# GpSimd's share of a sparse-attention stage: thresholds to VectorE, splits behind the masks, VectorE's order written out

## The chip, the cores and the metric

One Trainium2 chip, one core of it. The metric is the device time of one execution, in microseconds (us). The engines are TensorE (PE; its weight loads are listed apart as PEld), VectorE (DVE), ScalarE (ACT), GpSimd (POOL) and SyncE (SP), which issues most DMAs.

## The reference

Three stages follow one another. Attention over q, k, v of shape 4 batches x 8 heads x 576 tokens x 64, where each row of scores keeps only what lies within tau = 0.02 of its maximum:

```
scores = q @ k.T / sqrt(64)
thresh = max(scores, -1) - tau
scores = where(scores >= thresh, scores, -1e9)
attn   = exp(scores - max(scores, -1));  attn /= sum(attn) + 1e-9
x      = attn @ v                       # then 2304 tokens x 512
```

Then a gated stage, `(silu(x @ w_gate) * (x @ w_val)) @ w_out` with 1536 hidden columns, and a bilinear one, `((x @ w1) * (x @ w2)) @ w3 @ w_out2` with 1024. The change lies in attention.

## The kernel before, in words

**Precision.** TensorE runs on a rounded 32-bit type, so each operand is split into a high part (the rounded value) and a low part (the rest), and products are summed over two or three of the combinations. Many VectorE, ScalarE and GpSimd operations are such splits.

**Tiles.** Attention works on 16 head pairs (4 batches x 4), and in each on nine tiles of 128 query rows by 576 keys: four per head, and one (i = 4) that takes the last 64 rows of both heads. That makes 144 tiles, numbered n. For each tile:

- `mm_scores` (lines 426 to 444): four matmuls of 288 columns (eight for i = 4) into one of two score banks `s_bank`.
- `el_max` (475): VectorE negates the scores from the bank into the SBUF tile P and leaves their minimum (the negated maximum) in column c of `stat`.
- `el_thr` (466): GpSimd adds tau to that column. It does so for two tiles at a time (one for i = 4), 80 operations.
- `el_exp` (485): ScalarE makes E = exp(maximum - score) in one of three SBUF buffers (`N_E`).
- `el_mask` (494): VectorE compares P with the threshold, multiplies by E, writes P in place and sums it. It reads two SBUF tiles.

**Transposes.** When tile 4 and tile 8 of a pair are masked, items are queued (`a_items` 629, `b_items` 633): ten that transpose four blocks of P each into a PSUM bank (`it_T`, `it_lq`, `it_kl`), one for the corner, and four that multiply by V (`it_pv`). `evac_split` (506) takes a bank out by one of three paths, which `PATHS` (33) deals out in turn: X, high part by ScalarE and low part by VectorE, put off by one item through `deferred`; Z, high part by ScalarE, then TensorE subtracts it in the bank (`less`, 331) and ScalarE copies the low part; Y, ScalarE copies the bank into SBUF and GpSimd makes both parts (`split_pool`, 100: a rounding at line 101, a subtraction at 104).

**For the next pair**, items in the queue `prep` transpose k and q (`it_k`, `it_q`, through `turn`, 337: ScalarE's high part, VectorE's low part at 343, and then `stack`, 348, which issues SP DMAs into the tiles L and R that the scores read), and the last 64 rows (`it_left`, 407). GpSimd splits V (`split_v`, 301) and, once per batch, the last rows (`split_left`, 284).

**Order.** The loop at lines 705 to 741 goes tile by tile: exponential of n, maximum of n + 1, scores of n + 2, threshold of n, mask of n - 2 (`N_THR`), and between these `some` (693) runs items of the two queues, about two of `main` and one of `prep` per tile. This is only the order in which the program is written: a planner then orders each engine's instructions by their estimated costs and due times. In the last pair (`in_tail`) the path row is `LAST`, and the x loads of the gated stage (`x_prep`, 817) begin. In pairs 3, 6 and 9 (`EARLY`) one early weight unit is converted (`conv_bits` 132, `conv_value` 154), which takes ScalarE, GpSimd (line 151) and VectorE (158).

Of the kernel before, what the change touches and what calls it, by code (L numbers as in the profile page):

```python
# [29 lines left out]

PATHS, LAST = "XZYXZZYXZ", "XZ"


@with_exitstack
def kernel(
# [21 lines left out]
    nc = tc.nc  # L59
# [174 lines left out]
    def attention(actx, early, tail):  # L234
# [33 lines left out]
        def load(p, which):  # L268
            b, hp = divmod(p, HP)
            for i in which if p < NP else ():  # L270
# [10 lines left out]
                        nc.sync.dma_start(out=t, in_=src.rearrange("h (p t) d -> p t h d", t=4))  # L281
                raws[p, i] = t

        def split_left(b):
            qk, vl = lraw.pop(b)
            qks = sp.tile([P, H, 3, D], F32R, tag="qkls", name="qkls", bufs=1)
            eng = nc.gpsimd if b else nc.vector
            for e in (0, 2):
                eng.tensor_scalar(
                    out=qks[:, :, e, :], in0=qk, scalar1=1.0, scalar2=1.0,  # L290
                    op0=ALU.mult, op1=ALU.mult,
                )
            eng.tensor_tensor(
                out=qks[:, :, 1, :], in0=qk, in1=f32(qks[:, :, 0, :]), op=ALU.subtract
            )
            for h in range(2):
                r = slice(64 * h, 64 * h + 64)
                split_pool(VLZ[b % 2][r, :, h, 0, :], VLZ[b % 2][r, :, h, 1, :], vl[r])
# [38 lines left out]
        def turn(raw, hi, lo, scale, then):  # L337

            bank = t_bank()
            turn_p(bank, [raw[:, t, :, :].rearrange("p h d -> p (h d)") for t in range(4)])  # L340
            nc.scalar.activation(out=hi, in_=bank, func=ACTF.Copy, scale=scale)

            nc.vector.scalar_tensor_tensor(  # L343
                out=lo, in0=bank, scalar=scale, in1=f32(hi), op0=ALU.mult, op1=ALU.subtract
            )
# [60 lines left out]

        def it_left(p):
            b, hp = divmod(p, HP)
            L, R = qk_tiles(p)
# [12 lines left out]
            scaled(R[:, 512:640].rearrange("p (h c) -> p h c", h=2), bv[:, 1, :, 64:P])  # L422
            scaled(R[:, 2 * S:2 * S + 64], bv[:, 1, 1, 64:P])
# [70 lines left out]
        def el_mask(p, i, e):  # L494
            b = p // HP
            c = col_of(p, i)
            t = p_tile(p, i)
            nc.vector.scalar_tensor_tensor(  # L498
                out=t, in0=t, scalar=stats[b][:, 1, c:c + 1], in1=e, op0=ALU.is_le, op1=ALU.mult,
                accum_out=sums[b][:, c:c + 1],  # L500
            )
# [1 line left out]

        path_i = [0]

        def evac_split(hi, lo, bank):
            path = LAST[path_i[0] % len(LAST)] if in_tail else PATHS[path_i[0] % len(PATHS)]
            path_i[0] += 1
            if path == "Z":
                nc.scalar.copy(out=hi, in_=bank)  # L510

                def rest():
                    less(bank, hi)
                    nc.scalar.copy(out=lo, in_=bank)

                deferred.append(rest)
            elif path == "X":
                nc.scalar.copy(out=hi, in_=bank)
                deferred.append(
                    lambda: nc.vector.tensor_tensor(  # L520
                        out=lo, in0=bank, in1=f32(hi), op=ALU.subtract
                    )
                )
            else:
                raw = tmp()
                rv = raw
                if len(bank.shape) == 3:
                    rv = raw.rearrange("p (a c) -> p a c", a=bank.shape[1])
                if len(bank.shape) == 4:
                    rv = raw.rearrange("p (c h q) -> p c h q", c=4, h=2)  # L530
                nc.scalar.copy(out=rv, in_=bank)
                if path == "Y":
                    split_pool(hi, lo, rv)
                else:
                    nc.scalar.copy(out=hi, in_=bank)
                    nc.gpsimd.tensor_tensor(out=lo, in0=rv, in1=f32(hi), op=ALU.subtract)

        def it_T(p, h, c):
            bank = t_bank()
            o = 640 * h + c * P  # L540
            turn_p(bank, [pbuf[p, t][:, o:o + P] for t in range(4)])
            evac_split(AT[h][:, 0, c, 0:512], AT[h][:, 1, c, 0:512], bank)

        def it_lq(p):
            bank = t_bank()
            turn_p(bank, [pbuf[p, 4][:, c * P:(c + 1) * P] for c in range(4)])
            evac_split(
                *(ATT[:, :, e, :, 512:S].rearrange("p h c q -> p c h q") for e in range(2)),
                bank.rearrange("p (c h q) -> p c h q", c=4, h=2),
            )  # L550

        def it_kl(p):
            bank = t_bank()
            turn_p(bank, [pbuf[p, t][:, 512:640] for t in range(4)])
            evac_split(ATL[:, 0, 0:512], ATL[:, 1, 0:512], bank)

        def it_corner(p):
            bank = t_bank()
            nc.tensor.transpose(bank[:, 0:P], pbuf[p, 4][:, 448:S], ident)
            nc.tensor.transpose(bank[0:64, 64:64 + P], pbuf[p, 4][:, 512:S], ident)  # L560
            src, hi = bank[:, 64:P], ATL[:, 0, 512:S]
            nc.scalar.copy(out=hi, in_=src)
            nc.vector.tensor_tensor(
                out=ATL[:, 1, 512:S], in0=src, in1=f32(hi), op=ALU.subtract
            )

        xs_t = {}

        def it_pv(p, h, n):
            flush()  # L570
            b, hp = divmod(p, HP)
            vs = splits[p, 2]
            bank = t_bank()
            w = HALF
# [52 lines left out]
            return [lambda: split_left(p // HP)] if p % HP == 0 else []  # L627

        def a_items(p):
            r = [lambda: split_v(p)] + [lambda c=c: it_T(p, 0, c) for c in range(4)]  # L630
            return r

        def b_items(p):
            r = [lambda: it_kl(p), lambda: it_corner(p)]
# [45 lines left out]
                el_max(*tiles[n], banks.pop(n))  # L680

        def stage_mask(n):
            if n >= 0:
                p, i = tiles[n]
                el_mask(p, i, es.pop(n))
                if i == 4:
                    main.extend(a_items(p))
                if i == 8:
                    main.extend(b_items(p))

        credit = [0.0, 0.0]

# [6 lines left out]
                    run_item(qu.popleft())  # L699
                credit[c] = min(credit[c], 1.0)  # L700

        stage_s(0)
        stage_s(1)
        stage_max(0)
        for n, (p, i) in enumerate(tiles):
            b, hp = divmod(p, HP)
            if i == 0:
                if p + 2 < NP:
                    if (p + 2) % HP == 0:
# [4 lines left out]
                if p + 1 < NP:  # L714
                    prep.extend(prep_items(p + 1))
                    credit[1] = 0.0 if p else -1.5
            if i == NTILE - 2:
# [4 lines left out]
            some(0.4)  # L722
            es[n] = el_exp(p, i)
            stage_max(n + 1)
            stage_s(n + 2)
            el_thr(p, i)
            some(0.3)
            if n >= N_THR:
                stage_mask(n - N_THR)
            some(0.3)  # L730
# [6 lines left out]
            if n + 2 == NS:  # L737
# [4 lines left out]
        for n in range(NS - N_THR, NS):  # L742
# [6 lines left out]
        flush()  # L749

    make_identity(nc, ident)
    nc.vector.tensor_copy(out=ident_r, in_=ident)
# [373 lines left out]
```

## Time and profile before

| | us |
|---|---|
| median of 3 runs | 1181.99 |
| lowest and highest | 1175.48 to 1184.32 |
| the profiled execution: its span, the only time given of it | 1178.8 |
| VectorE busy in the span | 750.1 (64%) |
| TensorE busy in the span | 1113.3 (94%) |
| ScalarE, GpSimd busy in the span | 578.1 (49%), 439.7 (37%) |

The shares of the whole span mix attention (to some 365 us) with two stages of dense matrix work. How long an operation holds its engine is read from the distance between two starts: a VectorE operation and its follower overlap in the records, so durations add up to more than the time that passes.

### The profile page before, as it was taken

How to read it: one execution, taken by the hardware profiler on the slowest of the kernel's cores; microseconds unless marked ns; L12 is line 12 of the kernel's file. 1: busy time of each engine (PE TensorE's matmuls, PEld its weight loads, DVE VectorE, ACT ScalarE, POOL GpSimd, SP SyncE). 2: the span in 40 equal slices, each digit the busy share in tenths (PEclk: the TensorE clock that was granted, in tenths of full speed). 3: DMA queues.
4: the chain of work that ended last, by engine and by line, in shares of the span. 5: the costliest groups of instructions: out<-in, count | busy, mean ns of one | idle time of the engine just before them, and what ended most of it. 6: DMA issues, size and time to landing. Idle time of an engine off the chain costs nothing.

```text
span 1178.8 us, 16730 instructions
## 1 busy us (share of the span) xinstructions
PE 1113.3 (94%) x6044; PEld 952.0 (81%) x6044; DVE 750.1 (64%) x1320; ACT 578.1 (49%) x1041; POOL 439.7 (37%) x431
## 2 busy tenths in 40 slices
PE   6898879899988899999999999999899999999998
PEld 5787769788876778888888888888787888888886
DVE  7999898999886786665472655477891122522222
ACT  5787876888876455443232433344662231321111
POOL 4365454555444555443241432333242221321110
PEclk9999999999999999999999999999999999999999
DMA  8865674766555832221120120123330010100023
GB/s 189 194 146 131 145 177 112 167 147 137 121 175 141 257 99 87 89 72 55 35 71 19 54 72 19 52 92 102 113 108 18 1 36 1 36 1 1 1 60 101
DMA packets 105330, 107.07 MB, mean 91 GB/s; under 512 B 48288, under 2 KB 79648, under 8 KB 105248
## 3 DMA queue, kind: packets, MB, share of 16 engines
q1 hardware_dynamic: 105104, 106.01, 34.2%
q8 instruction: 47, 0.77, 0.3%
q14 instruction: 35, 0.29, 0.1%
q10 hardware_dynamic: 144, 0.00, 0.0%
HBM read 68.16 MB, written 14.23 MB: 70 GB/s over the span
## 4 chain that ended last, share of the span: by engine, by line
PE 64%; DVE 19%; DMA 8%; issue 3%; POOL 2%; SPq 2%; ACT 2%; DVEq 0%; ACTq 0%; POOLq 0%
PE t_bank L830 36%; PE s_bank L830 19%; DVE P L498 5%; DVE P L479 4%; PE t_bank L579 4%; PE s_bank L440 2%; DMA raw<-in_moe_w_dram 2%; DMA slot<-x_dram 1%; PE t_bank L326 1%; DVE slot L813 1%; DMA slot<-r_dram 1%; DVE tmp L158 1%; DVE tmp L146 1%; DVE AT L520 1%; DMA L<-qlo 1%
## 5 line engine op out<-in xcount | busy, mean ns | idle before, releaser
L830 PE MATMUL t_bank<-slot,slot 128*128 128x512 f32 (+1 forms) x2592 | 559.9, 371 | 5.6 <-DVE slot L813 1.8
L830 PEld LDWEIGHTS t_bank<-slot,slot 128*128 128x128 f32 x2592 | 457.5, 189 | 91.7 <-DVE slot L813 2.7
L830 PE MATMUL s_bank<-h,slot 128*128 128x512 f32 (+1 forms) x720 | 161.0, 371 | 7.4 <-DVE slot L877 4.2
L151 POOL TENSOR_TENSOR raw<-raw 128x512 int32<-128x512 int32 x76 | 83.9, 1104 | 189.0 <-ACT raw L150 165.3
L830 PEld LDWEIGHTS s_bank<-h,slot 128*128 128x128 f32 x720 | 126.4, 190 | 31.9 <-ACT tmp L914 3.2
L498 DVE SCALAR_TENSOR_TENSOR P<-P,stat,E 128x576 f32<-128x576 f32 x144 | 142.0, 999 | 11.8 <-POOL stat L471 10.6
L1062 DVE TENSOR_TENSOR tmp<-tmp,t_bank 128x512 f32<-128x512 f32 (+1 forms) x40 | 25.4, 634 | 178.3 <-PE t_bank L830 178.3
L488 ACT ACTIVATE E<-P,stat 128x576 f32<-128x576 f32 x144 | 113.6, 791 | 27.9 <-DVE P L479 25.2
L108 POOL TENSOR_TENSOR h<-tmp,h 128x512 fp32r<-128x512 f32 (+1 forms) x60 | 74.5, 1242 | 128.8 <-ACT h L107 128.6
L479 DVE TENSOR_SCALAR_CACHE_REDUCE P<-s_bank,neg 128x576 f32<-128x576 f32 x144 | 115.0, 808 | 10.3 <-PE s_bank L440 9.8
L1066 POOL TENSOR_TENSOR h<-tmp,h 128x512 fp32r<-128x512 f32 (+1 forms) x38 | 45.8, 1206 | 200.8 <-ACT h L1064 200.8
L440 PE MATMUL s_bank<-R,L 128*128 128x288 f32 x512 | 100.0, 317 | 19.3 <-DVE P L479 12.6
L830 PE MATMUL s_bank<-slot,h 128*128 128x512 f32 x432 | 106.6, 391 | 0.9 <-DVE slot L1052 0.8
L915 DVE TENSOR_TENSOR tmp<-tmp,t_bank 128x512 f32<-128x512 f32 (+1 forms) x60 | 37.9, 631 | 107.2 <-PE t_bank L830 100.5
L440 PEld LDWEIGHTS s_bank<-R,L 128*128 128x128 f32 x512 | 74.6, 191 | 33.8 <-DVE P L479 24.2
L326 PE MATMUL t_bank<-ident,P 128*128 128x128 f32 x640 | 91.4, 279 | 6.3 <-DVE klo L343 1.3
L830 PEld LDWEIGHTS s_bank<-slot,h 128*128 128x128 f32 x432 | 79.9, 188 | 18.3 <-DVE slot L1052 2.1
L158 DVE SCALAR_TENSOR_TENSOR tmp<-tmp,raw 128x512 f32<-128x512 f32 x76 | 69.5, 915 | 39.3 <-POOL raw L151 39.3
L877 DVE TENSOR_TENSOR slot<-s_bank,slot 128x1024 f32<-128x1024 f32 (+1 forms) x72 | 82.5, 1147 | 18.5 <-PE s_bank L830 16.5
L149 ACT ACTIVATE raw<-raw,ebias 128x512 int32<-128x512 int32 x76 | 58.0, 764 | 61.9 <-DVE tmp L146 48.2
L914 ACT ACTIVATE tmp<-t_bank 128x512 f32<-128x512 f32 (+1 forms) x60 | 33.3, 555 | 110.0 <-PE t_bank L830 104.3
L326 PEld LDWEIGHTS t_bank<-ident,P 128*128 128x128 f32 x640 | 74.3, 142 | 13.6 <-DVE klo L343 2.0
(103 smaller groups left out, 1397.8 us busy)
## 6 DMA issues: line engine op xcount, KB each, us to landing
raw<-in_moe_w_dram SPq DMA_DIRECT2D x32, 512.0 KB, 3.6
raw<-in_moe_w_out_dram SPq DMA_DIRECT2D x20, 512.0 KB, 3.6
x_dram<-xs SPq DMA_DIRECT2D x64, 144.0 KB, 2.4
L<-qlo SPq DMA_DIRECT2D x60, 128.0 KB, 2.4
L<-qhi SPq DMA_DIRECT2D x60, 128.0 KB, 4.0
raw<-in_moe_w_gate_dram SPq DMA_DIRECT2D x12, 512.0 KB, 4.3
raw<-in_moe_w_val_dram SPq DMA_DIRECT2D x12, 512.0 KB, 4.5
ld<-in_k_dram SPq DMA_DIRECT2D x16, 256.0 KB, 3.4
```

The lines of the kernel that those rows point to most:

```text
L108: nc.gpsimd.tensor_tensor(out=lo, in0=src, in1=f32(hi), op=ALU.subtract)
L149: nc.scalar.activation(out=a, in_=x, func=ACTF.Relu, scale=8.0, bias=ebias[:, 0:1])
L151: nc.gpsimd.tensor_tensor(out=a, in0=a, in1=x, op=ALU.subtract)
L158: nc.vector.scalar_tensor_tensor(out=f32(m), in0=f32(m), scalar=2.0 ** 20, in1=f32(a), op0=ALU.add, op1=ALU.mult)
L326: nc.tensor.matmul(bank[:, t * P:(t + 1) * P], lhsT=part, rhs=ident, is_transpose=True, start=(t == 0), stop=(t == len(parts) - 1),)
L440: nc.tensor.matmul(o, lhsT=lhs, rhs=R[:, c:c + HALF], start=(h == hs2[0] and e == 0), stop=(h == hs2[-1] and e == 1),)
L479: nc.vector.tensor_scalar(out=p_tile(p, i).rearrange("p (a c) -> p a c", a=2), in0=sb[:, :, 0:HALF], scalar1=neg, scalar2=None, op0=ALU.mu ...
L488: nc.scalar.activation(out=e, in_=p_tile(p, i), func=ACTF.Exp, scale=-1.0, bias=stats[p // HP][:, 0, c:c + 1],)
L498: nc.vector.scalar_tensor_tensor(out=t, in0=t, scalar=stats[b][:, 1, c:c + 1], in1=e, op0=ALU.is_le, op1=ALU.mult, accum_out=sums[b][:, c: ...
L579: nc.tensor.matmul(o, lhsT=vs[:, 4 * h + c, :, :].rearrange("p a d -> p (a d)"), rhs=AT[h][:, e, c, cs], start=(c == 0 and e == 0), stop=F ...
L830: nc.tensor.matmul(o, lhsT=lhs(a), rhs=rhs(c), start=(first and i == 0), stop=(last and i == 2))
L877: nc.vector.tensor_tensor(out=a, in0=s, in1=a, op=ALU.add)
```

## The change

- **Thresholds.** `el_thr` becomes one VectorE operation of one column for every tile (144).
- **Rounds of two tiles.** The loop goes in rounds: both maxima, both thresholds, both exponentials, the scores of the next two tiles, then the masks of the two tiles of the round before (`LAG` = 2). Items run before the maxima and on both sides of the masks, as many per tile as before.
- **VectorE's order.** Under `manual_schedule` VectorE runs in the order in which the program is written, from the first round until before the last pair; the planner still orders the other engines.
- **GpSimd's splits** are no longer issued where they arise but queued in `pool_q`, each with a cost. After the masks of a round, `pool_room` issues as many as fit in `ROOM` = 1.95 us, and each of these waits (by a semaphore) for the round's second mask. `pool_need` issues what is left, without that wait, before an item that reads it.
- **Paths.** Even pairs take YYZXZXZXZX, odd pairs YYZXZXZXZZ over their ten banks.
- **Low parts** of k and q (with their DMAs) and of the corner are put off by one item, as path X's already were. `split_v` moves from the first item of `a_items` to the start of its pair.

```diff
-N_THR, N_E = 2, 3
+LAG, N_E = 2, 3
+ROOM = 1.95
-PATHS, LAST = "XZYXZZYXZ", "XZ"
+PATHS, LAST = ("YYZXZXZXZX", "YYZXZXZXZZ"), "XZ"
...
+        def pool_next(gate=None):
+            _, cost, piece = pool_q.popleft()
+            made = piece()
+            if gate is not None and cost:
+                tc.add_manual_dep(
+                    made.ins, gate.ins.name,
+                    mybir.DependencyInfo(mybir.DependencyClass.Sync, mybir.DependencyReason.DATA),
+                    reason="behind the masks",
+                )
+        def pool_room(gate):
+            room = ROOM
+            while pool_q and pool_q[0][1] <= room:
+                room -= pool_q[0][1]
+                pool_next(gate)
+        def pool_need(*tags):
+            while any(t in tags for t, _, _ in pool_q):
+                pool_next()
+        def p_round(tag, hi, src, cost=0.62):
+            pool_q.append((tag, cost, lambda: nc.gpsimd.tensor_scalar(
+                out=hi, in0=src, scalar1=1.0, scalar2=1.0, op0=ALU.mult, op1=ALU.mult
+            )))
+        def p_rest(tag, lo, src, hi, cost=1.29):
+            pool_q.append((tag, cost, lambda: nc.gpsimd.tensor_tensor(
+                out=lo, in0=src, in1=f32(hi), op=ALU.subtract
+            )))
...
         def split_v(p):
-            split_pool(t[:, :, 0, :], t[:, :, 1, :], raw.rearrange("p h t d -> p (h t) d"))
+            p_round(("v", p), t[:, :, 0, :], src)
+            p_rest(("v", p), t[:, :, 1, :], src, t[:, :, 0, :])
             splits[p, 2] = t
-            load(p + 2, (2,))
+            pool_q.append((("v", p), 0.0, lambda: load(p + 2, (2,))))
...
-            nc.vector.scalar_tensor_tensor(
-                out=lo, in0=bank, scalar=scale, in1=f32(hi), op0=ALU.mult, op1=ALU.subtract
-            )
-            then()
+            def rest():
+                nc.vector.scalar_tensor_tensor(
+                    out=lo, in0=bank, scalar=scale, in1=f32(hi), op0=ALU.mult, op1=ALU.subtract
+                )
+                then()
+            deferred.append(rest)
...
-            if i in (0, 2, 5, 7):
-                return
-            c = slice(col_of(p, i) - (i != 4), col_of(p, i) + 1)
-            nc.gpsimd.tensor_scalar(
+            c = slice(col_of(p, i), col_of(p, i) + 1)
+            nc.vector.tensor_scalar(
                 out=st[:, 1, c], in0=st[:, 0, c], scalar1=tau_sb, scalar2=None, op0=ALU.add
             )
...
+        for n in round_of(0):
+            stage_s(n)
+        order = ExitStack()
+        order.enter_context(tc.manual_schedule(engines={mybir.EngineType.DVE}))
+        for n in range(0, NS, 2):
+            if n + NTILE + 1 == NS:
+                order.close()
+            for m in round_of(n):
+                begin_tile(m)
+            some(0.5)
+            for m in round_of(n):
+                stage_max(m)
+            for m in round_of(n):
+                el_thr(*tiles[m])
+            for m in round_of(n):
+                es[m] = el_exp(*tiles[m])
+            for m in round_of(n + 2):
+                stage_s(m)
+            some(0.75)
+            masks = [stage_mask(m) for m in round_of(n - LAG)]
+            if masks:
+                pool_room(masks[-1])
+            some(0.75)
+            for m in round_of(n):
+                end_tile(m)
```

Not shown: path Y and the splits of the last rows through the same two helpers, `pool_need("qk")` at the head of `it_left`, `pool_need(("v", p), ("vl", b), "at")` in `it_pv`, and the old loop's statements moved into `begin_tile` and `end_tile`.

## Rows read from the trace of the kernel before

**Rows 1.** Page, part 2: VectorE's busy tenths in 40 slices

```profile
DVE  7999898999886786665472655477891122522222
```

**Rows 2.** Table by stage: length, busy us of PE, PEld, DVE, ACT, POOL; PEclk, DMA, GB/s

```profile
38.10:348.00 309.90, 278.29 (x2009) 253.31 (x2009) 285.00 (x643) 249.91 (x499) 163.57 (x190) 0.99 0.63 147
...
450.00:1178.80 728.80, 719.17 (x3447) 604.39 (x3445) 357.18 (x499) 251.62 (x410) 210.41 (x176) 1.00 0.16 51
```

**Rows 3.** Line 479, maxima: ns shortest, median, longest; first and last start

```profile
L479 DVE TENSOR_SCALAR_CACHE_REDUCE P<-s_bank,neg x144: 800/807/819, 17.6 to 343.7; 128x576 f32<-128x576 f32 x144
```

**Rows 4.** Costliest groups, 30 to 330 us: busy us, mean ns, idle before and releasers

```profile
L498 DVE SCALAR_TENSOR_TENSOR P<-P,stat,E 128x576 f32<-128x576 f32 x132 | 130.8, 1003 | 10.1 <-POOL stat L471 8.9 <-ACT E L488 0.5 <-ACT xs L591 0.4
```

**Rows 5.** Line 498, masks, whole run, and what VectorE idled for before them

```profile
L498 DVE SCALAR_TENSOR_TENSOR P<-P,stat,E x144: 800/814/1931, 20.4 to 348.8; 128x576 f32<-128x576 f32 x144
...
  POOL stat L471: 10.6, 14
```

**Rows 6.** Timeline near 199 us: start, duration, engine, line, operation

```profile
198.28 0.81 DVE L479 TENSOR_SCALAR_CACHE_REDUCE P<-s_bank,neg 128x576 f32<-128x576 f32 x1
...
198.91 1.29 POOL L104 TENSOR_TENSOR AT<-tmp,AT 128x512 fp32r<-128x512 f32 x1
...
199.02 1.81 DVE L498 SCALAR_TENSOR_TENSOR P<-P,stat,E 128x576 f32<-128x576 f32 x1
```

**Rows 7.** Line 520, low parts of path X, whole run

```profile
L520 DVE TENSOR_TENSOR AT<-t_bank,AT x50: 628/680/692, 27.8 to 364.7; 128x512 fp32r<-128x512 f32 x50
```

**Rows 8.** Lines 101 and 104, GpSimd's splits of path Y, whole run

```profile
L101 POOL TENSOR_SCALAR AT<-tmp x29: 609/622/1192, 27.7 to 331.2; 128x512 fp32r<-128x512 f32 x29
...
L104 POOL TENSOR_TENSOR AT<-tmp,AT x29: 1272/1292/1892, 28.4 to 332.5; 128x512 fp32r<-128x512 f32 x29
```

**Rows 9.** Timeline, VectorE, near 5 us: an operation of one column and its follower

```profile
5.45 0.15 DVE L656 TENSOR_SCALAR neg<-tau_sb 128x1 f32<-128x1 f32 x1
5.51 0.69 DVE L392 TENSOR_SCALAR slot<-ld 128x256 fp32r<-128x256 f32 x3
```

**Rows 10.** Timeline, 211 to 217 us: q's high part, its low part and the follower

```profile
211.65 0.61 ACT L341 ACTIVATE qhi<-t_bank 128x512 fp32r<-128x512 f32 x1
...
216.35 0.68 DVE L343 SCALAR_TENSOR_TENSOR qlo<-t_bank,qhi 128x512 fp32r<-128x512 f32 x1
216.95 0.68 DVE L520 TENSOR_TENSOR ATL<-t_bank,ATL 128x512 fp32r<-128x512 f32 x1
```

**Rows 11.** Line 440, scores: what TensorE and its loads idled for (us, times)

```profile
  DVE P L479: 40.6, 72
  DMA L<-qlo: 5.2, 9
```

**Rows 12.** Timeline, ScalarE, near 301 us

```profile
300.78 0.78 ACT L488 ACTIVATE E<-P,stat 128x576 f32<-128x576 f32 x1
301.46 0.58 ACT L518 CAST AT<-t_bank 128x512 fp32r<-128x512 f32 x1
```

**Rows 13.** Timeline, TensorE, 226 to 229 us

```profile
226.48 1.03 PE L326 MATMUL t_bank<-ident,P 128*128 128x128 f32 x8
227.27 1.30 PE L440 MATMUL s_bank<-R,L 128*128 128x288 f32 x8
228.41 1.03 PE L326 MATMUL t_bank<-ident,P 128*128 128x128 f32 x8
```

**Rows 14.** VectorE's waits, whole run: us in total, times, longest

```profile
DVE P L479 <- PE s_bank L440: 9.8, 10, 1.9
...
DVE klo L343 <- ACT khi L341: 4.2, 1, 4.2
```

**Rows 15.** Timeline, GpSimd and VectorE, 91 to 94 us

```profile
91.59 1.60 POOL L104 TENSOR_TENSOR sp<-ld,sp 128x512 fp32r<-128x512 f32 x1
...
91.97 1.26 DVE L602 TENSOR_SCALAR r<-sums 128x36 f32<-128x36 f32 x1
93.27 0.38 DVE L605 RECIPROCAL r<-r 128x36 f32<-128x36 f32 x1
```

More of the change, by code (lines that the diff above doesn't have):

```diff
@@ L286, in split_left @@
             qks = sp.tile([P, H, 3, D], F32R, tag="qkls", name="qkls", bufs=1)
[L287 to L291, printed above, removed]
-                )
-            eng.tensor_tensor(
-                out=qks[:, :, 1, :], in0=qk, in1=f32(qks[:, :, 0, :]), op=ALU.subtract
-            )
+            if b:
+                for e in (0, 2):
+                    p_round("qk", qks[:, :, e, :], qk)
+                p_rest("qk", qks[:, :, 1, :], qk, qks[:, :, 0, :])
+            else:
+                for e in (0, 2):
+                    nc.vector.tensor_scalar(
+                        out=qks[:, :, e, :], in0=qk, scalar1=1.0, scalar2=None, op0=ALU.mult
+                    )
+                nc.vector.tensor_tensor(
+                    out=qks[:, :, 1, :], in0=qk, in1=f32(qks[:, :, 0, :]), op=ALU.subtract
+                )
             for h in range(2):
                 r = slice(64 * h, 64 * h + 64)
-                split_pool(VLZ[b % 2][r, :, h, 0, :], VLZ[b % 2][r, :, h, 1, :], vl[r])
+                hi, lo = (VLZ[b % 2][r, :, h, e, :] for e in range(2))
+                p_round(("vl", b), hi, vl[r], 0.42)
+                p_rest(("vl", b), lo, vl[r], hi, 0.74)
             lsplit[b] = qks
@@ L408, in it_left @@
             b, hp = divmod(p, HP)
+            pool_need("qk")
             L, R = qk_tiles(p)
@@ L467, in el_thr @@
             st = stats[p // HP]
-            if i in (0, 2, 5, 7):
-                return
-            c = slice(col_of(p, i) - (i != 4), col_of(p, i) + 1)
-            nc.gpsimd.tensor_scalar(
+            c = slice(col_of(p, i), col_of(p, i) + 1)
+            nc.vector.tensor_scalar(
                 out=st[:, 1, c], in0=st[:, 0, c], scalar1=tau_sb, scalar2=None, op0=ALU.add
@@ L504, in attention, with evac_split @@
         path_i = [0]
-        def evac_split(hi, lo, bank):
-            path = LAST[path_i[0] % len(LAST)] if in_tail else PATHS[path_i[0] % len(PATHS)]
+        def evac_split(p, hi, lo, bank):
+            row = LAST if in_tail else PATHS[p % 2]
+            path = row[path_i[0] % len(row)]
             path_i[0] += 1
@@ L531, in evac_split @@
                 nc.scalar.copy(out=rv, in_=bank)
[L532 to L536, printed above, removed]
+                p_round("at", hi, rv)
+                p_rest("at", lo, rv, hi)
         def it_T(p, h, c):
@@ L541, in it_T @@
             turn_p(bank, [pbuf[p, t][:, o:o + P] for t in range(4)])
-            evac_split(AT[h][:, 0, c, 0:512], AT[h][:, 1, c, 0:512], bank)
+            evac_split(p, AT[h][:, 0, c, 0:512], AT[h][:, 1, c, 0:512], bank)
         def it_lq(p):
@@ L547, in it_lq @@
             evac_split(
-                *(ATT[:, :, e, :, 512:S].rearrange("p h c q -> p c h q") for e in range(2)),
+                p, *(ATT[:, :, e, :, 512:S].rearrange("p h c q -> p c h q") for e in range(2)),
                 bank.rearrange("p (c h q) -> p c h q", c=4, h=2),
@@ L554, in it_kl @@
             turn_p(bank, [pbuf[p, t][:, 512:640] for t in range(4)])
-            evac_split(ATL[:, 0, 0:512], ATL[:, 1, 0:512], bank)
+            evac_split(p, ATL[:, 0, 0:512], ATL[:, 1, 0:512], bank)
         def it_corner(p):
@@ L629, in a_items @@
         def a_items(p):
-            r = [lambda: split_v(p)] + [lambda c=c: it_T(p, 0, c) for c in range(4)]
-            return r
+            return [lambda c=c: it_T(p, 0, c) for c in range(4)]
         def b_items(p):
@@ L682, in stage_mask @@
         def stage_mask(n):
[L683 to L689, printed above, removed]
+            p, i = tiles[n]
+            made = el_mask(p, i, es.pop(n))
+            if i == 4:
+                main.extend(a_items(p))
+            if i == 8:
+                main.extend(b_items(p))
+            return made
         credit = [0.0, 0.0]
@@ L700, in some, with begin_tile @@
                 credit[c] = min(credit[c], 1.0)
[L702 to L706, printed above, removed]
+        def begin_tile(n):
+            p, i = tiles[n]
             if i == 0:
@@ L721, in attention, with end_tile @@
                     prep.extend(split_items(p + 2))
[L722 to L730, printed above, removed]
+        def end_tile(n):
+            p, i = tiles[n]
             if i == 4 and p in EARLY:
@@ L741, in attention, with round_of @@
                 prep.extend(tail())
-        for n in range(NS - N_THR, NS):
+        def round_of(n):
+            return [m for m in (n, n + 1) if 0 <= m < NS]
+        for n in round_of(0):
[23 more added lines that the diff above has]
+                end_tile(m)
+        for n in range(NS - LAG, NS):
             stage_mask(n)
@@ L749, in attention @@
         flush()
+        assert not pool_q
     make_identity(nc, ident)
```

12 lines of the change are left out of this document (8 added, 4 removed).

## The prediction

> **What bounds the kernel now.** I read the page's slices first, then a table by stage, the costliest VectorE groups, and single stretches of the timeline. The slices show VectorE at nine tenths or near it through attention, the first twelve slices, and at a half or less behind it [rows 1]. The stage table says the same: from 38.1 to 348.0 us VectorE is busy 285.0 of 309.9 us, TensorE 278.3, ScalarE 249.9, GpSimd 163.6; behind 450 us TensorE is busy 719.2 of 728.8 [rows 2]. So the change, which touches attention alone, is worth what it takes off VectorE's time there, until TensorE takes over. The 144 maxima start from 17.6 to 343.7 us [rows 3]: 326.1/143 = 2.28 us per tile, 20.5 us per head pair of nine tiles.
>
> The second thing to see is that the masks are longer than they need be. 132 of them have a mean of 1003 ns [rows 4], but the median of all is 814 and the shortest 800 [rows 5]; the maxima, of the same 576 columns, lie between 800 and 819 [rows 3]. The long ones lie beside GpSimd: a mask that starts at 199.02, 0.11 us after a GpSimd subtraction of 1.29 us, lasts 1.81 us and ends 0.6 us after that subtraction does [rows 6]. The mask reads two SBUF tiles (P and E); the low-part subtractions read a PSUM bank, as the maxima do, and keep to 628 to 692 ns through all of this [rows 7]. Third, VectorE stood 14 times, 10.6 us in all, for the threshold that GpSimd computes [rows 5].
>
> **The change part by part.** The sum is made against the profiled span of 1178.8 us, beside which no other time of that execution is given; the median of the three runs is 3.2 us above it, and is what I forecast.
>
> *Masks free of GpSimd.* The splits are released by the second mask of a round and take 0.62 + 1.29 us [rows 8]. VectorE then does two maxima at a step of 0.74 us (198.28 to 199.02) [rows 6], the subtractions that are due, and two thresholds: at least 1.5 us of work that the rows show undisturbed. The stretch above the median goes: 144 x (1003 - 814) ns = 27.2 us. Bounds: 0, if the splits slip into the next masks again, and 27. I take 27, since 1.91 us of splits meet at least 1.5 us of cover and in most rounds a subtraction besides.
>
> *The wait for GpSimd's threshold* goes entirely: 10.6 us. Late next is E from ScalarE, for which a mask stood once in attention, 0.5 us [rows 4]; a mask now comes a whole round behind its exponential.
>
> *144 thresholds on VectorE*, one column each. A row of that size on VectorE lasts 0.15 us but takes a step of 0.06 (5.45 to 5.51) [rows 9]. Low end 144 x 0.06 = 8.6 us. The high end is a threshold that waits for its own accumulator and takes its full 0.15 us: 21.6. I take 0.08 us, near the row, since the second maximum lies between the first threshold and its accumulator: 11.5 us added.
>
> *Paths.* Three or four of ten banks take path X where three of nine did: 3.5 against 3.33 per pair, 0.17 x 16 x 0.60 us (a low part's step, 216.35 to 216.95 [rows 10]) = 1.6 us more on VectorE. ScalarE's copies stay the same within 0.1 per pair.
>
> *Low parts of k, q and the corner put off by one item*, and with k and q the 12 DMAs that their stack calls issue on SP. One item is some 0.7 us (2.28 us per tile, some three items). But before, the planner let a low part lie: qhi's copy began at 211.65 and took 0.61 us, and qlo started at 216.35, 4.1 us after its end [rows 10]. The fixed order puts it one item behind. Bounds: 15 x 0.7 = 10 us lost, if the scores wait for L in each pair, and 5 us gained, what TensorE stood for L [rows 11]. I take 0.
>
> *The new waits.* Behind a gated split on GpSimd lie the later splits and the weight conversion's subtractions, and for these a VectorE operation (line 158) whose place is now fixed. There are three such conversions inside attention: bounds 0 and 3 x 4 us (a round each); I take 2, nearer to nothing because a split is over in 1.9 us. The v split's customer, P times V, comes some two rounds later than the split. The v load on SP moves with its split, earlier; nothing waits for it. On ScalarE, three E buffers now hold the two tiles still to be masked and one new one: the second exponential of a round waits for the round's first mask, and what is queued behind it (copies of banks) waits with it. By steps ScalarE needs 9 exponentials at a step of 0.68 us (300.78 to 301.46) and 16.5 copies at 0.48 (the same 0.10 us of overlap off their 0.58) [rows 12], four of about 0.29 and 0.7 us of small ones per pair: 15.9 us, 3.5 per round of two tiles, in a cadence of 4.2. Up to 0.7 us per round is hidden; the wait is 0 where the planner puts copies ahead of the exponential, and some 0.9 us where it doesn't (second maximum's end to the mask's end, 0.15 + 0.74). I take 0 and keep 72 x (0.9 - 0.7) = 14 us as its upper end.
>
> *What TensorE gives back.* Its steps: transposes 0.10 us (eight from 226.48 to 227.27), scores 0.14 (eight from there to 228.41) [rows 13]; by their columns P times V 0.14 as well and the corrections of path Z 0.14 x 512/288 = 0.25 (estimates). Per pair 50 x 0.10 + 80 x 0.14 + 4.5 x 0.25 + 0.4 for the left block = 17.7 us. VectorE by steps, before: 18 x 0.74 + (3.33 + 2) x 0.60 + 0.14 = 16.7, with the masks' 1.7 and the waits' 0.7 19.1 of the 20.5; 1.4 is norms, conversions and other waits. After: 16.8 + 0.7 for thresholds + 1.4 = 18.9. TensorE's share of the cadence rises from 86% to 94%. VectorE stood 9.8 us for score banks at the lower share [rows 14]; I add half again, 5 us.
>
> Sum: 27 + 10.6 - 11.5 - 1.6 - 0 - 2 - 0 - 5 = 17.5 us saved. I take attention's end to be passed on whole: from 450 us on TensorE is full, and the loads between are started by attention's end. 1178.8 - 17.5 = 1161.3, and with 3.2 us **1164.5 us**.
>
> **A rule that speaks against it.** The norm's first operation, a VectorE tensor_scalar from SBUF to SBUF of 36 columns, took 1.26 us at 91.97, until a GpSimd split that began at 91.59 was over, and its follower started at its end [rows 15]. The Trainium skill, page "SBUF — State Buffer", section "Who interferes with whom", says that a tensor_scalar between SBUF tiles can enter a mode that takes the port pair shared with GpSimd for the whole instruction, and that whoever comes second stands still. The row agrees for 36 columns; no row has one column beside a split. By the rule the thresholds would stand, and the time would be the second rival's.
>
> **The rivals.**
> 1. *TensorE takes it back.* For it: scores waited 40.6 us for maxima [rows 11], so the two are closely coupled; against it: a bank is now asked for a round ahead. If VectorE stands 0.25 us more per round, 72 x 0.25 = 18 us; with the 5 already counted 13 more: 1177.
> 2. *Thresholds stand behind splits,* as the norm's operation did. They come 1.5 us behind the release in a round without a subtraction between, and splits last until 2.0 or so: up to 0.5 us in the 56 rounds that carry a split (3.5 per pair), 28 us at most; in half of them a subtraction has used that time up. Of the 14 us left some would have been waiting anyway: 10 us, 1174.
> 3. *Slower: the fixed order.* A subtraction whose copy is late now holds everything behind it on VectorE, where the planner would have moved a maximum forward; and the copy is late where it is queued behind the second exponential. The longest wait for a copy was 4.2 us, though a single one, at the start [rows 14]. One of 0.6 us in each of 72 rounds costs 43 us: 1164.5 + 43 = 1207. It decides from 17.5/72 = 0.24 us per round. Against it: the copy has an item's time, 0.7 us, for its 0.6.
> 4. *More than forecast.* If thresholds cost their step alone, half of the 1.4 us of other waits goes and TensorE keeps up, a pair takes 16.8 + 0.5 + 0.7 = 18.0 instead of 20.5 us: 16 x 2.5 = 40 us, 1142.
>
> **How the numbers follow.** Forecast 0.45 (its own range 1152 to 1172), rival 1 0.17, rival 2 0.13, rival 3 0.15, rival 4 0.10. What a measurement of this kernel can tell from no change is about 1%, so 1170 to 1194 is the same. Faster: nearly all of the forecast, rival 4 and a third of rival 2's spread, 0.59; within 1%: rival 1 and most of rival 2, 0.26; slower: rival 3, 0.15. The range holds rivals 1 and 2 and the ends of the unknown costs, and leaves out most of rival 3 and half of rival 4: 1142 to 1186.
>
> **What would show it.** Right: masks with a mean below 850 ns; no GpSimd thresholds and no wait of a mask for GpSimd; 144 thresholds of 0.15 us or less; the maxima from first to last in some 308 us instead of 326.1; splits at 0.62 and 1.29 us; at most 15 us of waits of maxima for score banks. Wrong: thresholds of 0.5 us beside splits (rival 2), waits for banks above 25 us (rival 1), subtractions that wait for ScalarE in most rounds (rival 3), or masks still near 1.0 us, in which case the gate does not do what it says.

## The result: slower by 0.6%, and the profile after

The changed kernel takes 1189.04 us (1186.75 to 1191.43) against 1181.6 us before: a ratio of 1.0063, with an interval of 1.0052 to 1.0073. That is within the 1% that my prediction counts as no change, but it lies on the side that I had not forecast and above the end of my range, 1186. The profiled span is 1185.6 us.

The three groups of VectorE in the profile after, by line (ns shortest, median, longest; first and last start). Line 521 is the maxima [rows 3], 540 the masks [rows 5], 513 the thresholds:

```profile
L521 DVE TENSOR_SCALAR_CACHE_REDUCE P<-s_bank,neg x144: 797/810/820, 15.4 to 355.2; 128x576 f32<-128x576 f32 x144
...
L540 DVE SCALAR_TENSOR_TENSOR P<-P,stat,E x144: 799/809/1851, 18.9 to 361.3; 128x576 f32<-128x576 f32 x144
...
L513 DVE TENSOR_SCALAR stat<-stat,tau_sb x144: 195/206/212, 16.9 to 359.7; 128x1 f32<-128x1 f32 x144
```

From the first maximum to the last pass 339.8 us, where 326.1 passed before. A table of just these stretches (length, then busy us of PE, PEld, DVE, ACT, POOL) tells where the 13.7 us came from. The kernel before:

```profile
17.60:343.70 326.10, 290.93 (x2076) 261.63 (x2076) 302.88 (x685) 261.58 (x519) 167.84 (x197) 0.99 0.65 150
```

and after:

```profile
15.40:355.20 339.80, 301.64 (x2120) 272.96 (x2118) 301.76 (x833) 267.81 (x526) 117.75 (x126) 0.96 0.64 148
```

VectorE's busy time is the same, 302.9 and 301.8 us. Its idle time rose from 23.2 to 38.0 us, by 14.8. So two things went wrong at once: the work taken off it came back as other work, and it now stands (waits for an input) longer.

The work came back as thresholds. The timeline of one round, GpSimd's row put among VectorE's:

```profile
217.12 1.29 POOL L313 TENSOR_TENSOR AT<-tmp,AT 128x512 fp32r<-128x512 f32 x1
...
217.12 0.81 DVE L521 TENSOR_SCALAR_CACHE_REDUCE P<-s_bank,neg 128x576 f32<-128x576 f32 x1
...
217.85 0.33 DVE L513 TENSOR_SCALAR stat<-stat,tau_sb 128x1 f32<-128x1 f32 x2
218.10 0.68 DVE L563 TENSOR_TENSOR AT<-t_bank,AT 128x512 fp32r<-128x512 f32 x1
```

Two thresholds take 0.25 us from start to the follower's start, 0.125 each, and 144 of them 18 us. The masks gave 144 x (999 - 839) ns = 23.0 us (the pages' means over all 144), so the gate did what it says; a few late masks, which run beside GpSimd's work for the gated stage (line 883, held by no gate), are still up to 1.85 us long. Two more low parts on path X (58 for 56) and conversions that now meet GpSimd take most of the rest.

The idle time shows in the list of waits from 30 to 330 us (who waited for whom: us in total, times, longest):

```profile
DVE P L521 <- PE s_bank L484: 16.8, 24, 3.8
ACT E L530 <- DVE P L540: 15.5, 17, 4.3
...
DVE AT L563 <- ACT AT L561: 9.0, 9, 1.9
...
PEld t_bank L462 <- POOL qkls L313: 8.1, 3, 2.8
...
DVE klo L384 <- ACT khi L381: 4.6, 4, 1.2
DVE tmp L159 <- POOL raw L152: 3.8, 3, 2.7
...
DVE slot L201 <- ACT slot L198: 2.3, 1, 2.3
```

VectorE stood for GpSimd's threshold before [rows 4]; that is gone. In its place it stands for score banks (16.8 us in this stretch), for ScalarE's copies (9.0 + 4.6) and for the early conversions (3.8 + 2.3). The second line is the wait that I had put at nothing: ScalarE holds the second exponential of a round until a mask frees an E buffer. The fourth is TensorE standing for the last rows' splits, which sit in the queue behind the masks.

Why a copy is late shows in path X's longest wait of this stretch: ScalarE works without a break, and an exponential and another copy stand ahead of the copy that is waited for.

```profile
264.13 0.85 ACT L530 ACTIVATE E<-P,stat 128x576 f32<-128x576 f32 x1
264.81 0.65 ACT L553 CAST AT<-t_bank 128x512 fp32r<-128x512 f32 x1
265.27 0.67 ACT L561 CAST AT<-t_bank 128x512 fp32r<-128x512 f32 x1
...
265.98 0.69 DVE L563 TENSOR_TENSOR AT<-t_bank,AT 128x512 fp32r<-128x512 f32 x1 [1.92 <-ACT AT L561]
```

The worst place is in pair 6, where an early conversion runs. Its steps in the timeline, [idle before <- releaser] at the end:

```profile
156.20 1.04 POOL L152 TENSOR_TENSOR raw<-raw 128x512 int32<-128x512 int32 x1 [4.72 <-ACT raw L151]
...
157.27 0.69 DVE L159 SCALAR_TENSOR_TENSOR tmp<-tmp,raw 128x512 f32<-128x512 f32 x1 [2.75 <-POOL raw L152]
...
159.57 0.63 ACT L198 CAST slot<-tmp 128x512 fp32r<-128x512 f32 x1
160.23 1.09 DVE L201 TENSOR_TENSOR slot<-tmp,slot 128x512 fp32r<-128x512 f32 x1 [2.27 <-ACT slot L198]
...
162.12 1.52 PE L484 MATMUL s_bank<-R,L 128*128 128x288 f32 x8 [2.10 <-DVE P L521]
165.31 2.29 PE L484 MATMUL s_bank<-R,L 128*128 128x288 f32 x8 [1.67 <-DVE P L521]
```

VectorE waits 2.75 us for GpSimd and 2.27 for ScalarE with its maxima and masks queued behind; TensorE then stands 2.10 and 1.67 us, and 2.18 more for the last rows at 169.78. Eight matmuls in 2.29 us, where the line above has 1.52, show the second cost, the clock; the table's granted clock is the third number from the end:

```profile
160.00:165.00 5.00, 1.54 (x9) 1.12 (x8) 4.77 (x12) 3.22 (x6) 1.17 (x2) 0.94 0.97 232
165.00:170.00 5.00, 2.51 (x10) 2.17 (x10) 5.00 (x15) 1.81 (x3) 2.35 (x4) 0.50 0.96 207
170.00:175.00 5.00, 5.00 (x26) 4.93 (x26) 4.11 (x13) 2.37 (x6) 1.95 (x4) 0.54 0.64 140
```

At 0.50 TensorE runs at 1.2 of its 2.4 GHz, for almost 10 us, behind 5 us in which it was busy 1.54. In the kernel before, the lowest 5 us of attention are these:

```profile
295.00:300.00 5.00, 3.87 (x21) 3.41 (x21) 5.00 (x14) 3.97 (x9) 1.41 (x2) 0.77 0.94 203
```

Not all of attention's 13.7 us reach the end: the last maximum starts 11.5 us later, the span is 6.8 us longer. By then TensorE had done 2165 matmuls where it had done 2122 before; behind that point it is busy 811.0 us instead of 813.8 and idle 19.4 instead of 21.3. Over the whole span TensorE's idle time is the same before and after, 65.5 and 65.6 us (span less busy time). What the span gained is, but for 0.1 us, TensorE's busy time for the same 6044 matmuls, 6.7 us more, at a lower mean granted clock. Busy times of the two pages and the clock of the whole span, before and then after:

```profile
PE 1113.3 (94%) x6044; PEld 952.0 (81%) x6044; DVE 750.1 (64%) x1320; ACT 578.1 (49%) x1041; POOL 439.7 (37%) x431
core 0: 1178.8 us, clock 0.994
...
PE 1120.0 (94%) x6044; PEld 959.4 (81%) x6044; DVE 744.0 (63%) x1466; ACT 580.9 (49%) x1041; POOL 381.3 (32%) x347
core 0: 1185.6 us, clock 0.984
```

So at the end the loss shows as longer busy time of TensorE, not as idle time. That the clock alone makes it was not tried apart.

### The profile page after: what moved, and what is told of

It is laid out like the page before. It is cut to its first block, busy times and chain, and to the rows that moved or that the text cites. A ratio compares the mean times of both kernels' runs of the same rounds, so it can differ in the third digit from the quotient of the medians.

```text
span 1185.6 us, 16777 instructions
## 1 busy us (share of the span) xinstructions
PE 1120.0 (94%) x6044; PEld 959.4 (81%) x6044; DVE 744.0 (63%) x1466; ACT 580.9 (49%) x1041; POOL 381.3 (32%) x347
## 4 chain that ended last, share of the span: by engine, by line
PE 67%; DVE 16%; DMA 6%; ACT 4%; issue 3%; SPq 3%; POOL 1%; DVEq 0%; ACTq 0%; POOLq 0%
PE t_bank L892 36%; PE s_bank L892 19%; PE t_bank L620 5%; DVE P L540 4%; PE s_bank L484 3%; DVE P L521 2%; PE t_bank L366 2%; DVE slot L875 2%; DMA raw<-in_moe_w_dram 2%; DVE tmp L159 1%; SPq L852 1%; PE t_bank L625 1%; ACT E L530 1%; DMA slot<-r_dram 1%; DVE raw L144 1%
## 5 line engine op out<-in xcount | busy, mean ns | idle before, releaser
L521 DVE TENSOR_SCALAR_CACHE_REDUCE P<-s_bank,neg 128x576 f32<-128x576 f32 x144 | 112.7, 811 | 21.8 <-PE s_bank L484 21.8
L540 DVE SCALAR_TENSOR_TENSOR P<-P,stat,E 128x576 f32<-128x576 f32 x144 | 116.0, 839 | 0.0
L366 PE MATMUL t_bank<-ident,P 128*128 128x128 f32 x640 | 98.6, 282 | 12.9 <-DVE P L540 4.1
L484 PE MATMUL s_bank<-R,L 128*128 128x288 f32 x512 | 98.2, 319 | 11.5 <-DVE P L521 7.8
L484 PEld LDWEIGHTS s_bank<-R,L 128*128 128x128 f32 x512 | 76.8, 196 | 19.0 <-DVE P L521 13.7
```

The costliest lines, as they stand in the source:

```text
L366: nc.tensor.matmul(bank[:, t * P:(t + 1) * P], lhsT=part, rhs=ident, is_transpose=True, start=(t == 0), stop=(t == len(parts) - 1),)
L484: nc.tensor.matmul(o, lhsT=lhs, rhs=R[:, c:c + HALF], start=(h == hs2[0] and e == 0), stop=(h == hs2[-1] and e == 1),)
L521: nc.vector.tensor_scalar(out=p_tile(p, i).rearrange("p (a c) -> p a c", a=2), in0=sb[:, :, 0:HALF], scalar1=neg, scalar2=None, op0=ALU.mu ...
L540: return nc.vector.scalar_tensor_tensor(out=t, in0=t, scalar=stats[b][:, 1, c:c + 1], in1=e, op0=ALU.is_le, op1=ALU.mult, accum_out=sums[b ...
```

## The experiments

Ratios are to the kernel before, run beside on the same chip; a difference between two kernels is the difference of their ratios times 1182 us. One caution holds for all: the planner plans the other engines anew for every edit, so each edit shifts more than its own operations, and a difference of 4 us or so from a single edit isn't a clean price for its part.

**1. Parts undone.** Thresholds alone, put into the kernel before:

```diff
-            if i in (0, 2, 5, 7):
-                return
-            c = slice(col_of(p, i) - (i != 4), col_of(p, i) + 1)
-            nc.gpsimd.tensor_scalar(
+            c = slice(col_of(p, i), col_of(p, i) + 1)
+            nc.vector.tensor_scalar(
```

> The kernel before with one part of the change alone: 144 one-column thresholds on VectorE, the planner's order kept. Theory T (thresholds cost about their measured step of 0.125 us, 18 us, and give back GpSimd's interference and waits): masks still near 1.0 us beside splits but fewer of them, VectorE's wait for GpSimd's threshold (10.6 us) gone; time within 5 us of before, either way. Theory O (the fixed order alone costs): thresholds are harmless, and this is faster than before by 8 us or more.

1187.53 us, ratio 1.0054 (1.0036 to 1.0072): 6 us slower. Masks fell only to 935 ns, and the thresholds, whose step is again 0.12 us (63.95 to 64.07), are work:

```profile
L496 DVE SCALAR_TENSOR_TENSOR P<-P,stat,E 128x576 f32<-128x576 f32 x130 | 120.5, 935 | 2.5 <-ACT E L486 2.3
...
L469 DVE TENSOR_SCALAR stat<-stat,tau_sb 128x1 f32<-128x1 f32 x130 | 25.1, 203 | 0.0
```

```profile
63.34 0.68 DVE L518 TENSOR_TENSOR AT<-t_bank,AT 128x512 fp32r<-128x512 f32 x1
63.95 0.20 DVE L469 TENSOR_SCALAR stat<-stat,tau_sb 128x1 f32<-128x1 f32 x1
64.07 0.81 DVE L496 SCALAR_TENSOR_TENSOR P<-P,stat,E 128x576 f32<-128x576 f32 x1
```

So thresholds on VectorE cost time in the kernel before too, a little over the 5 us of theory T. Little of it is seen in attention: in the profiled execution, 10.5 us longer than the one before, the maxima pass in 329.3 us, 3.2 more, with VectorE busy 313.5 us, 10.6 more, and idle 15.8, 7.4 less. The rest lies behind the last maximum and is not accounted for. The changed kernel with `nc.gpsimd` in that operation:

> The changed kernel with the thresholds back on GpSimd, one column each. Theory T: VectorE loses 144 x 0.125 = 18 us of work, so 10 to 18 us faster than the changed kernel, 1171 to 1179. Theory O (the fixed order's stands decide): the stands stay, VectorE only waits longer at the same places, gain under 5 us.

1187.94 us, 1.0055 (1.0042 to 1.0068): 1 us faster, no more. VectorE's busy time from 30 to 330 us fell from 263 to 251 us, after first and then this run:

```profile
30.00:330.00 300.00, 268.92 (x1896) 245.09 (x1897) 263.22 (x731) 238.35 (x472) 101.61 (x110) 0.96 0.63 146
```

```profile
30.00:330.00 300.00, 271.61 (x1912) 248.12 (x1913) 251.18 (x613) 238.58 (x474) 158.37 (x235) 0.96 0.63 146
```

but the time did not follow. In the changed kernel VectorE's work is no longer the bound; theory T falls there, and the order's stands are left. The changed kernel without its order:

```diff
-        order.enter_context(tc.manual_schedule(engines={mybir.EngineType.DVE}))
```

> The changed kernel without the fixed order of VectorE; rounds, gates and thresholds stay. Theory O: the waits of VectorE for ScalarE's copies, for conversions and for score banks (38 us in 30 to 330 us) fall by a third or more, and the time by 8 us or more. Theory T: within 4 us of the changed kernel. Theory G (the gate makes GpSimd late, above all for the last rows' split of each batch): within 4 us too, and the three waits of TensorE for that split stay.

1175.32 us, 0.9946 (0.9928 to 0.9964): 14 us faster than the changed kernel and 6 us faster than before. The maxima now take 315.8 us:

```profile
16.40:332.20 315.80, 287.82 (x2062) 262.88 (x2061) 306.81 (x826) 260.15 (x516) 129.39 (x124) 0.98 0.66 151
```

VectorE is busy 306.8 us, 5 more than with the fixed order, since masks are back at 904 ns, and idle 9.0 instead of 38.0. The stretch is 24.0 us shorter than under the fixed order, and some 14 of these reach the end: theory O. And the gate taken out of the changed kernel, `pool_room(None)` for `pool_room(masks[-1])`:

> The changed kernel without the semaphore that holds the splits behind the masks; queue and room stay. Theory G: TensorE's waits for the last rows' split (2.2 to 2.5 us, three times) and the low clock behind them go, 5 to 10 us faster than the changed kernel although masks get longer. If the gate is worth what I forecast: masks back above 0.9 us and 10 us or more slower.

1206.36 us, 1.0209 (1.019 to 1.0227): 17 us slower than with the gate, as the last sentence had it:

```profile
L540 DVE SCALAR_TENSOR_TENSOR P<-P,stat,E 128x576 f32<-128x576 f32 x117 | 108.5, 962 | 0.0
```

The rounds, the paths and the put-off low parts of k and q were not undone by themselves.

**2. Where the fixed order stands.** Last rows' q and k splits issued at once on GpSimd (the three `p_round` and `p_rest` calls in `split_left` replaced by the operations themselves):

> The changed kernel with the last rows' q and k splits (once per batch) issued at once on GpSimd instead of through the queue behind the masks. Theory Q (the queue makes these splits late, TensorE stands 2.2 to 2.5 us in three places and runs on at the low clock): the waits of the left block's transposes for GpSimd fall below 3 us in all (15.2 in the changed kernel), the granted clock in 30 to 330 us rises from 0.96 towards 0.98, 3 to 8 us faster than the changed kernel, 1181 to 1186. Rival (what they cost is regained, since VectorE is behind anyway): under 2 us.

1185.53 us, 1.0022 (1.001 to 1.0034): 5 us faster than the changed kernel. The waits for these splits are gone from the list. Path X's low part put off by two items:

```diff
+        def twice(f):
+            deferred.append(lambda: deferred.append(f))
...
-                deferred.append(
+                twice(
```

> The changed kernel with the low part of path X put off by two items instead of one, in the same fixed order. Theory H (a late copy holds VectorE's whole queue): the waits of path X's subtractions for ScalarE (9 us in 30 to 330 us) fall below 3 us and the time by 4 to 8 us, 1181 to 1185. Rival B (banks): each bank is held an item longer, transposes wait for it, and the time is the same or longer by up to 5 us.

1184.32 us, 1.0025 (1.0008 to 1.0041): 4.5 us faster; the waits of path X's subtractions fell from 9.0 to 4.6 us, not below 3. But those of the corner's low parts, still put off by one item, rose from 0.2 to 4.3, and the maxima take 339.7 us, as in the changed kernel:

```profile
16.30:356.00 339.70, 305.72 (x2120) 275.73 (x2118) 304.64 (x835) 269.00 (x528) 117.81 (x126) 0.96 0.63 148
```

So the gain is not in that stretch, and theory H is not shown by it. Four E buffers, which need room, and the control for the room:

```diff
-LAG, N_E = 2, 3
+LAG, N_E = 2, 4
-N_TMP, N_BIG, N_HB = 6, 3, 3
+N_TMP, N_BIG, N_HB = 5, 3, 3
```

> The changed kernel with four E buffers instead of three; to make room, five scratch tiles instead of six. Theory E (the second exponential of a round waits for the round's first mask and holds ScalarE's queue, so copies come late): ScalarE's waits for masks (18.7 us) go, with them half or more of VectorE's waits for ScalarE, 5 to 12 us faster than the control with five scratch tiles. Rival: the planner had put copies ahead, ScalarE only idles elsewhere, within 3 us of the control.

> Control: the changed kernel with five scratch tiles instead of six and nothing else. Within 4 us of the changed kernel if scratch tiles are not short; slower by more if they are, and then only the difference to the run with four E buffers counts.

1195.06 us (1.0111, 1.0092 to 1.0131) against the control's 1187.03 (1.0043, 1.0026 to 1.0059): a fourth E buffer costs 8 us. (The control itself is 2.4 us faster than the changed kernel, an example of the caution above.) The waits of ScalarE and VectorE with four:

```profile
DVE AT L563 <- ACT AT L561: 12.5, 16, 1.7
DVE klo L384 <- ACT khi L381: 10.2, 5, 2.0
...
ACT E L530 <- DVE P L521: 39.1, 33, 2.9
```

and ScalarE's in the control:

```profile
ACT E L530 <- DVE P L540: 18.0, 21, 2.6
ACT E L530 <- DVE P L521: 15.1, 19, 1.7
```

The wait for masks went, and the exponentials waited 39.1 us for maxima instead: ScalarE took them up too early, and the copies behind them came later still, 22.7 us of VectorE's waits where the control has 13.1. Theory E falls. That the buffer's wait, unmeant, kept copies ahead of exponentials fits this, but was not tried apart. The conversion moved by `EARLY = (3, 7, 9)`:

> The changed kernel with the second early weight conversion in pair 7 instead of 6. In pair 6 VectorE's fixed order stood 2.75 us for GpSimd's subtraction and 2.27 us for ScalarE's copy, TensorE stood 2.1 and 1.7 us behind it and ran at the low clock for 10 us. Theory C (the place in pair 6 is unlucky: an even pair, where a round ends between the conversion's steps): the first wait falls below 1 us as in pairs 3 and 9 (0.4, 0.6), 3 to 8 us faster than the changed kernel. Rival: the chain itself costs (value on VectorE, copy on ScalarE, low part on VectorE again, with nothing between in the fixed order), so the second wait stays at 2 us and the time within 3 us.

1183.31 us, 1.0005 (0.9991 to 1.0019): 7 us faster, 4.2 of them in the stretch of the maxima (335.6 us). Both waits nearly went, not the first alone:

```profile
DVE tmp L159 <- POOL raw L152: 1.4, 3, 0.6
...
DVE slot L201 <- ACT slot L198: 0.7, 1, 0.7
```

All three mends (without the E buffer):

> The changed kernel, its fixed order kept, with three mends at once: last rows' splits issued at once, path X's subtractions two items late, second early conversion in pair 7. If the fixed order's cost of 14 us lies in these places and they add up: 1177 to 1181, the time of the kernel before. If the order costs everywhere, a little in each round: 1183 or more.

1178.71 us, 0.9968 (0.9953 to 0.9984): 11 us faster than the changed kernel, where the three alone add up to 16. The stretch of the maxima shows what they do in attention:

```profile
16.40:348.30 331.90, 302.98 (x2121) 268.80 (x2119) 306.99 (x836) 268.83 (x528) 118.13 (x126) 0.98 0.65 151
```

It is 7.9 us shorter, and VectorE is idle 24.9 us, where the planner's order made it 24.0 shorter, with 9.0 idle. So the three places hold about a third of what the order costs in attention. That the rest is spread over the rounds, as the second expectation has it, is not ruled out.

**3. With the planner's order.** Thresholds on GpSimd, and the same with the last rows at once:

> Rounds, gate and paths of the change, but the planner's order on VectorE and thresholds on GpSimd (one column each). If the cost of thresholds on VectorE is real where VectorE is the bound (6 us when done alone), this is 3 to 8 us faster than the run with the planner's order and thresholds on VectorE: 1168 to 1173. If waits of masks for GpSimd come back, as the 10.6 us of before, it is the same or slower, 1175 to 1182.

> The same with the last rows' splits issued at once as well. If that part is worth 4 us here too (as in the fixed order): 1164 to 1169. If it was worth something only because the fixed order left nothing to slip forward: within 2 us of the run without it.

1186.66 us (1.0034, 1.0016 to 1.0051) and 1184.69 (1.001, 0.9993 to 1.0027). A miss: thresholds on GpSimd are 10 us slower here than on VectorE, where alone they had been 6 us faster. Waits of masks for GpSimd came back, but only 2.8 us of them; the maxima's waits for score banks rose more, from 6.8 to 19.0 us, and why stays open. The last rows at once are worth 2.8 us here, between the two expectations. Without the gate:

> Rounds and thresholds of the change, planner's order on VectorE, no gate on the splits. If the gate frees the masks whoever orders VectorE: masks back near 1.0 us (0.90 with the gate), 8 to 17 us slower than with the gate, 1184 to 1192. If the planner's order undoes the gate anyway (it puts other masks behind the released splits, mean 904 ns against 822): within 3 us, 1173 to 1179.

1174.25 us, 0.9948 (0.9927 to 0.9968): the same as with it, though masks are at 947 ns:

```profile
L540 DVE SCALAR_TENSOR_TENSOR P<-P,stat,E 128x576 f32<-128x576 f32 x144 | 135.3, 947 | 0.5 <-ACT E L530 0.5
```

The maxima pass in 320.9 us, 5.1 more than with the gate, but this does not reach the end. So at the end the gate is worth 17 us under the fixed order and nothing under the planner's, where masks are at 904 ns even with it. Thresholds merged, in the mended fixed order:

```diff
-            for m in round_of(n):
-                el_thr(*tiles[m])
+            el_thr(*(tiles[m] for m in round_of(n)))
```

> The fixed order with its three mends, and the two thresholds of a round as one operation where their columns touch (about 90 in place of 144). 54 x 0.125 = 7 us less on VectorE. If VectorE bounds once the stands are mended: 4 to 7 us faster than the mended run, 1172 to 1175. If its time is filled by waits for banks and copies instead, as when the thresholds went back to GpSimd: within 2 us, 1177 to 1181.

1182.79 us, 1.0006 (0.9987 to 1.0025): 4.5 us slower than the mended run, outside both expectations. The two shapes of the threshold, by mean ns (second number):

```profile
L528 DVE TENSOR_SCALAR stat<-stat,tau_sb 128x2 f32<-128x2 f32 x56 | 20.1, 359 | 1.9
...
L528 DVE TENSOR_SCALAR stat<-stat,tau_sb 128x1 f32<-128x1 f32 x32 | 5.4, 206 | 0.0
```

Two columns stand beside a split where one column doesn't. In the timeline of this run a threshold ends with GpSimd's subtraction:

```profile
96.95 1.30 POOL L313 TENSOR_TENSOR AT<-tmp,AT 128x512 fp32r<-128x512 f32 x1
...
97.60 0.67 DVE L528 TENSOR_SCALAR stat<-stat,tau_sb 128x2 f32<-128x2 f32 x1
...
98.19 0.81 DVE L556 SCALAR_TENSOR_TENSOR P<-P,stat,E 128x576 f32<-128x576 f32 x1
```

The maxima pass in 332.2 us, in the mended run in 331.9, so the 4.5 us are not traced to these stands. Last, two sums of parts under the planner's order: last rows and conversion; and all mends with merged thresholds.

> The planner's order with the gate, thresholds on VectorE, last rows' splits issued at once and the second early conversion in pair 7. If those two parts cost whoever orders VectorE: 3 to 8 us faster than the planner's order alone, 1167 to 1172. If they cost only because the fixed order held everything behind them: within 3 us, 1172 to 1178.

1167.59 us, 0.9891 (0.9866 to 0.9915): the fastest, 13 us under the kernel before and 20 under the changed one. Its two mends are worth 6.5 us with no fixed order either, so they are not the order's cost alone. Its maxima start from 16.0 to 333.0 us, 317.0 where the planner's order alone has 315.8, so the 6.5 us lie outside that stretch; where is open.

> The planner's order with all mends: last rows at once, path X two items late, conversion in pair 7, merged thresholds. If VectorE is the bound of attention here, the 7 us of merged thresholds come off on top: 1162 to 1169. If not: 1170 to 1178.

1187.45 us, 1.0056 (1.0037 to 1.0074): a miss, 20 us above the run before it and 9 above its higher expectation. Its 56 two-column thresholds take 398 ns on average, 11 us more in all than at 203; why the rest is lost (later low parts, another plan) is open.

## Why the prediction was wrong

- *Masks.* Right in mechanism and nearly in size: 23 us against 27.
- *The wait for GpSimd's threshold.* Right: no wait of a mask for GpSimd is left.
- *Thresholds.* The first step that failed, by size: 0.08 us taken, 0.125 measured, 18 us against 11.5. The thresholds show 206 ns where the row it leaned on [rows 9] has 149. A wait for the accumulator, which was my high end, is not the reason: in the run with thresholds alone, many stand behind another operation than their maximum (the three lines above) and take the same 0.20 us and step. That row also differs in its scalars, which are numbers, where the threshold reads tau from SBUF; whether this is the reason was not tried.
- *Low parts behind one item, new waits, TensorE.* The step that decided. I wrote 0 for the low parts, 2 us for the conversions, 0 for ScalarE and 5 for TensorE. Instead, VectorE's idle time rose by 14.8 us although 10.6 us of waits had gone: some 25 us of new stands. The argument that "the copy has an item's time, 0.7 us, for its 0.6" counted the copy and left out what lies ahead of it on ScalarE (264 to 266 us above). The order's price is 14 us at the end, by the run without it, and 24.0 in the stretch of the maxima; the three mends of last rows, copies and one conversion bring back 7.9 of these 24.0, and where the rest lies is not shown.
- *The rivals.* The third had the mechanism, at 14 us rather than 43: from 30 to 330 us VectorE stood for ScalarE's copies of path X and k 13 times, not in every round. The second fell for one column: no threshold is longer than 212 ns, though the timeline above has two beside a split. The first came in part: maxima waited 21.8 us for banks against 9.8 before [rows 14], under my mark of 25 but above the 15 of a right forecast; in pair 6 TensorE itself had waited for VectorE, the other waits were not taken apart.
- *Passing it on.* I took attention's end to be passed on whole. It was not: 11.5 us later at the last maximum, 6.8 at the end. Nor had the sum a term for TensorE's clock, whose mean fell from 0.994 to 0.984.

## What to carry to other kernels

An order written out for one engine turns each late input into a stand for all that follows it, and its price is not in that engine's busy time: compare idle time in the same stretch, and list what each operation waits for through the queue of the engine that makes it, not by its own duration. Before writing out an order, mend the inputs that come late (here one split in a queue and one conversion's place: with them the planner's order came to 0.9891, below every fixed one tried). Work taken off contended operations is won only if what comes in exchange costs less, so price it from a row of the same operation with the same operands, not merely the same shape.

## What the runs showed that I had not expected

- A tensor_scalar of one column on VectorE, SBUF to SBUF, was not disturbed by GpSimd's splits (144 of them, 195 to 212 ns, of which 57 start while a split runs); of two columns it was, up to 1248 ns with the fixed order and 1348 with the planner's. The Trainium skill, page "Vector Engine (DVE) Microarchitecture Reference", section "5.1 Performance modes — why throughput varies by op and dtype", says that two elements per partition with one source in SBUF run in a mode that uses both read ports. The two-column rows (mean 359 ns against 206) agree with that, and one column behaves as an operation outside it; no run here shows the mode itself.
- One more buffer made the kernel 8 us slower: the engine that had waited for it then waited longer, at another place.
- TensorE's granted clock was 0.50 (1.2 GHz) from 165 to 170 us, after 5 us in which it was busy 1.54; before, the lowest such value in attention was 0.77, and over the whole span TensorE is idle no longer than before but busy 6.7 us longer.
